# Five PSUM banks in turn for the first-layer sums of an mLSTM and mixture-of-experts kernel

## The chip, the cores and the metric

The kernel runs on one core of a Trainium2 chip. The metric is the device time of one launch in microseconds. A profile comes from one further execution, recorded by the hardware profiler; its span reaches from the first to the last instruction of the core.

## The reference

An mLSTM (4 batches, 8 heads, 768 steps, head size 40) makes 3072 rows of 320 numbers, and a mixture of eight experts is applied to them. Cut to what matters here:

```python
x = attn_out.transpose(0, 2, 1, 3).reshape(B * S, H * D)      # 3072 x 320
expert_idx = argmax(normalised(x) @ normalised(emb).T / tau)   # one expert for each row
for e in range(8):
    mask = expert_idx == e
    h = np.maximum(x[mask] @ w1[e], 0.0)                       # 320 -> 1024, first layer
    out[mask] = gate_w[mask, None] * (h @ w2[e])               # 1024 -> 320, second layer
```

## The kernel before

The order of the instructions on each engine is the order in the source: nothing is reordered, and semaphores are set from the tiles that are read and written. The mLSTM takes about the first third of the span. The expert stage follows; only the mLSTM's last steps overlap it.

**Precision.** Every float32 operand is split into a high and a low part (names ending in `h` and `l`). A product is the sum of three matmuls: high by high, low by high, high by low.

**The stages of the experts.** Two experts are chosen early from a sample. Their tokens come in two lists of 256 each: the first lists (tiles named `_a`) are worked on while the routing still goes on, the second lists (`_b`, 256 columns for each of the two experts) afterwards. The six later experts follow one by one, with 448, 448, 384, 384, 320 and 320 columns. For each expert:

- `gather` has GpSimd fetch the token rows by an indirect DMA (line 322); ScalarE doubles the last 64 columns (`double`, line 352).
- `x_chunk` turns 128 of the row's columns at a time: TensorE transposes (line 360) into a PSUM tile `pt`, ScalarE copies the high part (lines 363, 366), VectorE makes the low part (lines 364, 367). There are three chunks for an expert.
- `mm1` makes one 128-wide slice of the hidden layer: eight matmuls (line 397) into a PSUM tile `ph`, then ScalarE's ReLU into `hh` (line 399), then VectorE's rest into `hl` (line 401, and 405 for an odd half tile). The bank of `ph` comes free after VectorE's instruction. There are eight slices for an expert.
- `mm2` makes the second layer of 128 tokens: 24 matmuls (line 435, or 16 of line 422 for a last half tile) into `po`, scaled by VectorE (line 451) and scattered by GpSimd (line 454).

**The second lists.** While the second layer of the first lists runs, the three turned chunks of the second lists are put between its matmuls, and `g_sums` (line 526) sums the gates in a tile of pool `pM`, which VectorE reads with three instructions (lines 535 to 537). Then sixteen calls of `mm1` follow, eight for each of the two experts. VectorE gets the ordering of the later experts' lists between them, and one-element memsets (line 171) that release the loads of the next expert's weights. Then come four tiles of the second layer, with casts of the next expert's weights (line 208 on ScalarE, line 211 on VectorE) and its turned chunks between them.

**The PSUM pools.** There are eight banks: `pX` has one, `pM` two, `pO` two for `po`, `pH` three for `ph`. `pX` served the mLSTM's transposes and one early tile of the experts and is not used afterwards. `pM` served the routing sums and serves `pt`. Each pool gives its banks out in turn, and an instruction that writes a bank waits until the last reader of its previous tile is done. The lines of the change's inner part are these:

```python
pt = pM.tile([P, 512], F32, name="pt", tag="pm")                                   # x_chunk
ph = pH.tile([P, 512], F32, name="ph", tag="ph")[:, 0 : xc.stop - xc.start]        # mm1
```

Of the kernel before, what the change touches and what calls it, by code (L numbers as in the profile page):

```python
# [11 lines left out]
F32 = mybir.dt.float32  # L12
# [14 lines left out]
P = 128  # L27
# [39 lines left out]
def tile_mlstm_moe(  # L67
# [159 lines left out]
    pX = mctx.enter_context(tc.tile_pool(name="pX", bufs=1, space=PSUM))  # L227
    pM = mctx.enter_context(tc.tile_pool(name="pM", bufs=2, space=PSUM))
# [86 lines left out]
        return [[lambda f=f: next(f)] * k for f, k in parts]  # L315


    pp = []

    def gather_rows(xs, cols, rows=NT + 1):  # L320
        for a, c in enumerate(cols):
# [27 lines left out]
    def double(xs, a, w=P):  # L349

        n = -(-w // P)
        A.copy(xs[:, a : a + n, DM:XW], xs[:, a : a + n, 2 * P : DM])

    def x_chunk(x, xs, c, w=CAP):
        xh, xl, xt = x
        if c == 0:
            double(xs, 0, w)
        pt = pM.tile([P, 512], F32, name="pt", tag="pm")
        for a in range(0, w, P):
            T.transpose(pt[:, a : a + P], xs[:, a // P, c * P : (c + 1) * P], ident)  # L360
        pt = pt[:, 0:w]
        if c < 2:
            A.copy(xh[:, c, 0:w], pt)
            V.tensor_tensor(xl[:, c, 0:w], pt, xh[:, c, 0:w].bitcast(F32), ALU.subtract)
        else:
            A.copy(xt[:, 0:w], pt)
            V.tensor_tensor(xt[L:P, 0:w], pt[L:P], xt[L:P, 0:w].bitcast(F32), ALU.subtract)
# [14 lines left out]
    def hidden(nm):  # L382
        hh, hl = [], []
        for f in range(FC):
            hh.append(mp.tile([P, CAP], F32R, name=f"hh_{nm}_{f}", tag="hh", bufs=FC + 1))
            hl.append(mp.tile([P, CAP], F32R, name=f"hl_{nm}_{f}", tag="hl", bufs=FC + 1))
        return hh, hl

    def mm1(ws, x, xc, f, hs, hc):
        w1h, w1l, (xh, xl, xt) = ws["w1h"], ws["w1l"], x  # L390
        fs = slice(f * P, (f + 1) * P)
        ph = pH.tile([P, 512], F32, name="ph", tag="ph")[:, 0 : xc.stop - xc.start]
        ops = [(w[:, c, fs], xh[:, c, xc]) for c in range(2) for w in (w1h, w1l)]
        ops += [(w1h[:, c, fs], xl[:, c, xc]) for c in range(2)]
        ops += [(w[:, 2, fs], xt[:, xc]) for w in (w1h, w1l)]
        for i, (lt, rh) in enumerate(ops):
            T.matmul(ph, lt, rh, start=i == 0, stop=i == len(ops) - 1)  # L397
        hh, hl = hs[0][f][:, hc], hs[1][f][:, hc]
        A.activation(hh, ph, AF.Relu)  # L399
        full = (hc.stop - hc.start) // P * P  # L400
        V.scalar_tensor_tensor(  # L401
            hl[:, 0:full], ph[:, 0:full], 0.0, hh[:, 0:full].bitcast(F32), ALU.max, ALU.subtract
        )
        if hc.stop - hc.start > full:
            V.scalar_tensor_tensor(
                hs[0][f][:, hc.stop : hc.stop + L], ph[:, full:], 0.0, hh[:, full:].bitcast(F32), ALU.max, ALU.subtract
            )
# [137 lines left out]
    with ExitStack() as actx:  # L545
# [223 lines left out]
        def stage_store(n):  # L769
            j, b = divmod(n, B)  # L770
            SY.dma_start(xrows(j)[:, b], xs_[j][:, b])
# [680 lines left out]
        def do(k):  # L1452
            for _ in range(k):
                if todo:
                    todo.pop(0)()
# [7 lines left out]
        def first_hidden(e, f):  # L1463
            mm1(exps[e]["ws"], xa[e], slice(0, HALF), f, hs, slice(e * HALF, (e + 1) * HALF))
# [12 lines left out]
        n, g = NS - 1, len(GROUPS) - 1  # L1477
        yctx.close()
        pH = mctx.enter_context(tc.tile_pool(name="pH", bufs=3, space=PSUM))
        pp.append(mctx.enter_context(tc.tile_pool(name="pO", bufs=2, space=PSUM, side="right")))  # L1480
        stage_store(n)
        stage_xc(n)
# [26 lines left out]
        def first_out(i, po, ob=None):  # L1509
            e, a = divmod(i, HT)  # L1510
            mm2_out(po, gtf[:, e, a : a + 1], ida_v[i], f"a{i}", ob)
# [51 lines left out]
    for f in g_split:  # L1563
        f()
    xp = x_tiles(mp, "p", CAP)
    xps = [lambda c=c: x_chunk(xp, xs, c) for c in range(3)]
    po2 = first_sum(2, {}, True)
    po3 = first_sum(3, {14: xps[0], 18: xps[1], 22: xps[2]})
# [16 lines left out]
    ranks, places, lists, list_gates, beyond = arrange(mp)  # L1585
    todo += ranks + places + [where] + lists + [tokens] + list_gates
    hs = hidden("b")
    for e in range(NE):
        for f in range(FC):
            mm1(exps[e]["ws"], xp, slice(e * HALF, (e + 1) * HALF), f, hs, slice(e * HALF, (e + 1) * HALF))  # L1590
            do(3 - e)
            if e * FC + f in W2_AT:
                exps[2]["load"](W2_AT.index(e * FC + f), V)()
            if f % 4 == 1:
                first_out(2 * e + f // 4, *first_outs[2 * e + f // 4])
        if e == 0:
            exps[2]["tiles"](wp, 1)
            todo += beyond
    xp = x_tiles(mp, "2", CAP)
    xps = [lambda c=c: x_chunk(xp, xs, c, CAPS[0]) for c in range(3)]  # L1600
    todo += [exps[2]["piece"](*p) for p in PIECES1]
    for i in range(NE * HT):
# [12 lines left out]
    for e in range(NE, E):  # L1615
# [3 lines left out]
        if e + 1 < E:  # L1619
            exp = exps[e + 1] = load_expert(e + 1, at[j + 1])  # L1620
            exp["tiles"](wq if e % 2 == 0 else wp, 1)
            exp["tiles"](w22[(e + 1) % 2], 2)
            todo += [exp["load"](i) for i in range(7)]
            todo += [exp["piece"](*p) for p in PIECES1 + PIECES2]
            n = CAPS[j + 1]
            xs = gather(ids_g[j + 1]) if j else xs_n
            xp = x_tiles(mp, e + 1, CAP)
            xps = [lambda c=c, xp=xp, xs=xs, n=n: x_chunk(xp, xs, c, n) for c in range(3)]
            do(7)
        hs = hidden(e)  # L1630
        for f in range(FC):
            mm1(ws, x, w, f, hs, w)
            do(1)
# [19 lines left out]
    with tc.If(over > 0):  # L1653
        with ExitStack() as octx:
# [49 lines left out]
            with tc.For_i(0, again, 1):  # L1704
                V.tensor_copy(expert, num)
                for n in range(NS):
# [14 lines left out]
                    px = pv.tile([P, 512], F32, name="ovt", tag="ovt")  # L1721
# [33 lines left out]
            with tc.For_i(0, E, 1) as k:  # L1755
# [10 lines left out]
                with tc.For_i(0, NS, 1) as t:  # L1766
# [10 lines left out]
                    pt = pv.tile([P, 512], F32, name="ovt", tag="ovt")  # L1777
# [6 lines left out]
                    for f in range(FC):  # L1784
                        ph = pv.tile([P, 512], F32, name=f"ovh_{f}", tag="ovh")
# [79 lines left out]
```

## Time and profile before

| what | us |
|---|---|
| median of three runs | 335.27 (334.59 to 336.45) |
| the profiled execution | 335.94 |
| its span, first to last instruction | 334.1 |
| TensorE busy in the span | 310.5 |
| VectorE busy | 218.4 |
| ScalarE busy | 162.6 |
| GpSimd busy | 146.8 |

In the rows below, PE is TensorE's matmuls, PEld its weight loads, DVE VectorE, ACT ScalarE, POOL GpSimd. An engine works its instructions off in order, so an instruction that waits holds up all behind it. The arrow in square brackets names what ended the idle time before an instruction, as inferred from semaphores. The end of a matmul in the profile is modelled.

### The profile page before, as it was taken

The page shows a single profiled execution, that of the slowest core. Times are in us where ns is not written, and L with a number is a line of the kernel's source. Part 1 is how long each engine was busy: PE and PEld are TensorE (multiplying, and loading weights), DVE is VectorE, ACT ScalarE, POOL GpSimd, SP SyncE. Part 2 cuts the span into 40 slices and gives each one's busy share as a digit, 9 for nine tenths or more (in the row PEclk, how much of TensorE's full clock was granted, in tenths as well). Part 3 has the DMA queues.
Part 4 walks back from the last instruction along what each step waited for, and adds up shares of the span by engine and source line. Part 5 has one row for each costly group of instructions (what it writes and reads, how often), then busy time and mean ns, then how long its engine had stood idle before and what let it go on. Part 6 is the DMA issues. An engine that isn't in the chain of part 4 may idle for free.

```text
span 334.1 us, 9812 instructions
## 1 busy us (share of the span) xinstructions
PE 310.5 (93%) x3768; PEld 293.1 (88%) x3769; DVE 218.4 (65%) x633; ACT 162.6 (49%) x429; POOL 146.8 (44%) x182
## 2 busy tenths in 40 slices
PE   8997999779987988999889999999999999999992
PEld 4787999769986788999889989999999999999992
DVE  6676797875884649896456596476566585685530
ACT  4666665545654493343245364354454464463410
POOL 6668766768777088040622611240260241332112
PEclk9999999998999899999979999999999999999999
DMA  7999888987998514020592977347347447430001
GB/s 231 278 329 292 260 271 258 344 271 222 284 301 228 204 55 125 2 80 1 186 265 69 257 253 203 110 125 212 118 120 228 126 141 229 115 103 34 17 13 46
DMA packets 29342, 58.54 MB, mean 175 GB/s; under 512 B 3851, under 2 KB 18392, under 8 KB 29286
## 3 DMA queue, kind: packets, MB, share of 16 engines
q1 hardware_dynamic: 26406, 48.91, 47.9%
q0 software_dynamic: 2624, 8.48, 8.4%
q8 instruction: 32, 0.52, 0.6%
q10 hardware_dynamic: 256, 0.43, 0.4%
q14 instruction: 24, 0.20, 0.2%
HBM read 49.98 MB, written 8.19 MB: 174 GB/s over the span
## 4 chain that ended last, share of the span: by engine, by line
PE 79%; DVE 4%; issue 4%; DMA 4%; ACT 3%; POOL 3%; another core or an unknown queue 1%; SPq 1%; POOLq 0%; DVEq 0%; ACTq 0%
PE ph L397 27%; PE po L435 17%; PE s L644 4%; PE po_b L435 4%; PE y L719 4%; PE po_a L435 4%; PE y L730 3%; PE y L681 3%; PE po L422 3%; PE pt L360 2%; DMA sig<-in_og 2%; PE warm L1083 2%; PE px L797 2%; DMA raw<-in_w 2%; PE pm L817 2%
## 5 line engine op out<-in xcount | busy, mean ns | idle before, releaser
L454 POOL DMA_INDIRECT out<-ob,ids x20 | 20.3, 1016 | 99.7 <-DVE ob L451 73.9
L629 POOL TENSOR_TENSOR uv<-kv_s,u_t 64x328 f32<-64x328 f32 x47 | 35.9, 764 | 12.2 <-PE y L681 5.0
L435 PE MATMUL po<-w2h,hh 128*128 128x320 f32 x128 | 40.3, 315 | 0.0
L399 ACT ACTIVATE hh<-ph 128x448 fp32r<-128x448 f32 (+2 forms) x48 | 23.6, 492 | 33.3 <-PE ph L397 31.6
L435 PE MATMUL po<-w2h,hl 128*128 128x320 f32 x128 | 39.6, 309 | 0.0
L435 PE MATMUL po<-w2l,hh 128*128 128x320 f32 x128 | 39.5, 309 | 0.0
L401 DVE SCALAR_TENSOR_TENSOR hl<-ph,hh 128x384 fp32r<-128x384 f32 (+1 forms) x48 | 24.6, 512 | 14.8 <-ACT hh L399 11.7
L397 PE MATMUL ph<-xh,w1h 128*128 128x448 f32 (+2 forms) x96 | 32.2, 338 | 0.1
L397 PE MATMUL ph<-xh,w1l 128*128 128x448 f32 (+2 forms) x96 | 32.1, 337 | 0.0
L208 ACT CAST w1h<-raw 128x512 fp32r<-128x512 f32 x48 | 28.8, 616 | 1.0 <-DMA raw<-in_w 1.0
L451 DVE TENSOR_SCALAR ob<-po,gts 128x320 f32<-128x320 f32 x16 | 8.8, 551 | 28.1 <-PE po L435 28.1
L211 DVE TENSOR_TENSOR w2l<-raw,w2h 128x320 fp32r<-128x320 f32 x58 | 26.5, 493 | 0.2
L644 PE MATMUL s<-q_s,k_e 128*64 128x64 f32 x384 | 24.3, 223 | 1.2 <-DVE w_s L653 1.0
L208 ACT CAST w2h<-raw 128x320 fp32r<-128x320 f32 x62 | 25.2, 461 | 0.0
L397 PE MATMUL ph<-xl,w1h 128*128 128x448 f32 (+2 forms) x96 | 24.6, 337 | 0.0
L322 POOL DMA_INDIRECT xs<-x_d,ids x20 | 21.4, 1071 | 6.9 <-issue 5.5
L211 DVE TENSOR_TENSOR w1l<-raw,w1h 128x512 fp32r<-128x512 f32 x36 | 24.4, 688 | 0.0
L644 PE MATMUL s<-q_s,k_o 128*64 128x64 f32 x384 | 24.2, 222 | 0.0
L435 PEld LDWEIGHTS po<-w2l,hh 128*128 128x128 f32 x128 | 24.1, 188 | 0.0
L653 DVE TENSOR_TENSOR w_s<-s,late 128x512 f32<-128x512 f32 x24 | 16.5, 686 | 11.7 <-PE s L644 7.1
L435 PEld LDWEIGHTS po<-w2h,hh 128*128 128x128 f32 x128 | 24.1, 188 | 0.0
L435 PEld LDWEIGHTS po<-w2h,hl 128*128 128x128 f32 x128 | 24.0, 188 | 0.0
(328 smaller groups left out, 928.9 us busy)
## 6 DMA issues: line engine op xcount, KB each, us to landing
raw<-in_w SPq DMA_DIRECT2D x32, 320.0 KB
kv_s<-in_rows SPq DMA_DIRECT2D x23, 324.0 KB
raw<-in_w SPq DMA_DIRECT2D x14, 512.0 KB
q_s<-in_qt SPq DMA_DIRECT2D x11, 512.0 KB
raw<-in_w SPq DMA_DIRECT2D x18, 256.0 KB
sig<-in_og SPq DMA_DIRECT2D x24, 160.0 KB
x_d<-x SPq DMA_DIRECT2D x24, 160.0 KB
k_e<-in_kt SPq DMA_DIRECT2D x11, 160.0 KB
```

Source lines behind the costliest of these rows:

```text
L208: A.copy(h, src)
L211: (eng or V).tensor_tensor(lo, src, h.bitcast(F32), ALU.subtract)
L322: G.indirect_dma_start(out=xs[0 : c.shape[0], a, 0:DM], out_offset=None, in_=x_d[0:rows], in_offset=bass.IndirectOffsetOnAxis(ap=c, axis=0 ...
L397: T.matmul(ph, lt, rh, start=i == 0, stop=i == len(ops) - 1)
L399: A.activation(hh, ph, AF.Relu)
L401: V.scalar_tensor_tensor(hl[:, 0:full], ph[:, 0:full], 0.0, hh[:, 0:full].bitcast(F32), ALU.max, ALU.subtract)
L435: T.matmul(po[0 : ts_.stop - ts_.start, 0:DM], lt[f][:, ts_], rh[:, f], start=k == 0, stop=k == len(ops) - 1)
L454: store = G.indirect_dma_start(out=out, out_offset=bass.IndirectOffsetOnAxis(ap=slots, axis=0), in_=ob, in_offset=None, bounds_check=NT - ...
L629: (eng[r] if eng else G).tensor_tensor(uv[n % NB][rows, :, :, r], vr_s[q % NB][rows, k], u_t[rows, j, b].unsqueeze(3).broadcast_to([L, 2, ...
L644: T.matmul(s[r * L : r * L + L, c, a], (k_e, k_o)[a % 2][q % NB][:, k, m, cs], q_s[q % NB][:, k, m, cs], start=True, stop=True,)
L653: V.tensor_tensor(w_s[n % NB].rearrange("p c a t -> p (c a) t"), st[n]["s"].rearrange("p c a t -> p (c a) t"), late.unsqueeze(1).broadcast ...
L719: T.matmul(y[c * L : c * L + L, a * 2 * D1 : (a + 1) * 2 * D1], w_s[n % NB][:, c, a], uv[n % NB][:, c, a].rearrange("p r d -> p (r d)"), s ...
```

## The change

`mm1` no longer takes its bank from `pH` alone but from a list that turns with every call. The list holds `pH` once until the second lists begin, so that the first lists have three banks as before; then `pH` is added twice and `pM` twice, which gives the order `pH`, `pH`, `pH`, `pM`, `pM`. `x_chunk` takes its bank from `pX` and `pM` in turn, beginning with `pX`. Nothing else is changed; no instruction of any engine is added or moved in the source.

```diff
-    pp = []
+    pp, banks = [], []
+    turns = [(pM, "pm"), (pX, "px")]
...
-        pt = pM.tile([P, 512], F32, name="pt", tag="pm")
+        turns.append(turns.pop(0))
+        pt = turns[0][0].tile([P, 512], F32, name="pt", tag=turns[0][1])
...
-        ph = pH.tile([P, 512], F32, name="ph", tag="ph")[:, 0 : xc.stop - xc.start]
+        pool, tag = banks[0]
+        banks.append(banks.pop(0))
+        ph = pool.tile([P, 512], F32, name="ph", tag=tag)[:, 0 : xc.stop - xc.start]
...
         pH = mctx.enter_context(tc.tile_pool(name="pH", bufs=3, space=PSUM))
+        banks.append((pH, "ph"))
...
     hs = hidden("b")
+    banks += [(pH, "ph")] * 2 + [(pM, "pm")] * 2
     for e in range(NE):
```

## Rows read from the trace of the kernel before

**Rows 1.** Busy time by engine: us, share of the span, instructions.
```profile
PE 310.5 (93%) x3768; PEld 293.1 (88%) x3769; DVE 218.4 (65%) x633; ACT 162.6 (49%) x429; POOL 146.8 (44%) x182
```

**Rows 2.** By stretch: us; busy (count) PE, PEld, DVE, ACT, POOL; clock, DMA share, GB/s.
```profile
178.00:308.00 130.00, 129.91 (x825) 127.15 (x824) 84.86 (x184) 63.16 (x144) 37.63 (x36) 1.00 0.53 153
```

**Rows 3.** Timeline of TensorE: start us, us, engine, line, what, idle before.
```profile
154.03 0.36 PE L397 MATMUL ph<-xh_p,w1h 128*128 128x256 f32 x1
...
162.41 0.28 PE L397 MATMUL ph<-xt_p,w1l 128*128 128x256 f32 x1
...
163.37 0.28 PE L397 MATMUL ph<-xt_p,w1l 128*128 128x256 f32 x1
...
164.84 0.39 PE L397 MATMUL ph<-xh_p,w1h 128*128 128x256 f32 x1 [0.22 <-DVE hl_b L401]
...
168.48 0.39 PE L397 MATMUL ph<-xh_p,w1h 128*128 128x256 f32 x1 [2.42 <-DVE hl_b L401]
...
173.90 0.31 PE L435 MATMUL po_b<-w2h,hh_b 128*128 128x320 f32 x1
```

**Rows 4.** Timeline of ScalarE, same columns.
```profile
163.94 0.39 ACT L399 ACTIVATE hh_b<-ph 128x256 fp32r<-128x256 f32 x1 [1.77 <-PE ph L397]
167.58 0.94 ACT L399 ACTIVATE hh_b<-ph 128x256 fp32r<-128x256 f32 x3 [3.26 <-remote]
...
174.38 1.65 ACT L208 CAST w1h<-raw 128x512 fp32r<-128x512 f32 x3
175.93 0.40 ACT L352 COPY xs<-xs 128x256 f32<-128x256 f32 x1
```

**Rows 5.** Timeline of VectorE, same columns.
```profile
154.69 0.19 DVE L537 SCALAR_TENSOR_TENSOR gtf<-gtf,pg 128x32 f32<-128x32 f32 x1
...
164.36 0.42 DVE L401 SCALAR_TENSOR_TENSOR hl_b<-ph,hh_b 128x256 fp32r<-128x256 f32 x1 [1.74 <-ACT hh_b L399]
...
168.00 0.42 DVE L401 SCALAR_TENSOR_TENSOR hl_b<-ph,hh_b 128x256 fp32r<-128x256 f32 x1 [2.86 <-ACT hh_b L399]
...
169.06 0.42 DVE L401 SCALAR_TENSOR_TENSOR hl_b<-ph,hh_b 128x256 fp32r<-128x256 f32 x1
```

**Rows 6.** Timeline of GpSimd, same columns: the last of four gathers.
```profile
164.28 1.00 POOL L322 DMA_INDIRECT xs<-x_d,ids x1 [0.30 <-issue]
```

**Rows 7.** Pauses of TensorE and what follows them, columns as in rows 2.
```profile
70.40:72.40 2.00, 0.00 (x0) 0.00 (x0) 1.49 (x6) 0.98 (x4) 0.62 (x1) 1.00 0.83 262
73.60:76.90 3.30, 3.30 (x39) 2.85 (x36) 1.25 (x3) 1.71 (x6) 3.23 (x4) 0.50 0.88 308
105.60:107.60 2.00, 0.67 (x6) 0.32 (x4) 0.00 (x0) 0.12 (x1) 1.70 (x2) 1.00 1.01 193
107.70:111.10 3.40, 3.18 (x30) 2.74 (x31) 1.72 (x5) 0.48 (x2) 1.04 (x1) 0.50 1.06 357
119.10:120.30 1.20, 0.00 (x0) 0.00 (x0) 0.14 (x1) 1.20 (x4) 1.20 (x2) 1.00 0.00 0
120.40:124.40 4.00, 4.00 (x49) 3.97 (x50) 1.93 (x7) 3.97 (x14) 4.00 (x5) 1.00 0.06 10
...
166.10:168.40 2.30, 0.00 (x0) 0.00 (x0) 0.40 (x2) 0.82 (x3) 0.52 (x1) 1.00 1.01 341
169.20:172.50 3.30, 3.30 (x18) 3.30 (x17) 1.85 (x11) 0.77 (x2) 1.00 (x1) 0.50 0.80 181
```

**Rows 8.** Line 397 alone by stretch: us; busy PE, PEld; clock, DMA share, GB/s.
```profile
155.05:161.58 6.53, 6.53 (x58) 6.53 (x57) 1.00 0.07 26
168.48:172.95 4.47, 4.47 (x25) 4.47 (x26) 0.62 0.88 232
```

**Rows 9.** Timeline of TensorE around the gate sums, columns as in rows 3.
```profile
152.41 0.39 PE L435 MATMUL po_a<-w2h,hl_a 128*128 128x320 f32 x1
153.03 1.18 PE L526 MATMUL pg<-ag,op_all 128*128 128x96 f16 x24 [0.22 <-DVE xl_p L364]
```

**Rows 10.** Timeline of ScalarE in a later expert's first layer, columns as in rows 4.
```profile
295.24 0.44 ACT L399 ACTIVATE hh<-ph 128x320 fp32r<-128x320 f32 x1 [0.58 <-PE ph L397]
```

## The prediction

> **What bounds the kernel now.** I read the page's table of busy time first: TensorE is busy for 310.5 of 334.1 us [rows 1]. A share like that can hide where the rest went, so the second view was the busy time by stretch. From 178 to 308 us, which holds nearly all work of the later experts, TensorE is idle for 0.09 of 130 us at full clock [rows 2]: no bank, buffer or weight is waited for there, and a change that only gives room can win nothing in that stretch. The third view was TensorE's timeline around the one stage that the change touches and that has holes, the first-layer sums of the second lists (154 to 174 us). They are sixteen groups of eight matmuls, which I number 1 to 16 (1 to 8 are the first expert's, 9 to 16 the second's). Group 12 starts after a wait of 0.22 us and group 13 after one of 2.42 us, both ended by VectorE's `hl` of line 401 [rows 3], that is by a bank coming free: with three banks, group 12 needs the bank of 9, and 13 that of 10.
>
> The fourth and fifth views say why the banks came free late. The last matmul of group 9 starts at 162.41 and that of group 10 at 163.37, each 0.28 us long [rows 3]; ScalarE reads them at 163.94 and 167.58 [rows 4], 1.2 and 3.9 us after their ends. In those pauses ScalarE had nothing else queued, and at 167.58 it read three groups in 0.94 us: their sums had been there. VectorE follows at 164.36, 168.00 and 169.06 [rows 5]. So TensorE's completions of groups 9 to 12 were seen late. At that time GpSimd's gathers of rows, of which the last of four is issued at 164.28, are in flight [rows 6] and the DMA engines are full (share 1.01) [rows 7]; this is a coincidence in time, not a proven cause. After the long wait the granted clock is 0.50 from 169.2 to 172.5 [rows 7]. [...]
>
> What this stage loses: seven undisturbed groups (2 to 8) take 6.53 us, so 0.933 each [rows 8]. Sixteen from 154.03 would end near 169.1 (the first takes 1.02, to 155.05), and the second layer starts at 173.90 [rows 3]. That is 4.8 us: 0.4 before group 12, 2.6 before group 13, and 4.47 - 2.80 = 1.67 us for groups 13 to 15 at the low clock [rows 8], with 0.1 of small change.
>
> **The change part by part.** It adds and removes no operation on any engine and moves no DMA; it only renames PSUM banks, so what changes is what a group waits for.
>
> *Five banks for `ph` in the second lists.* The ring is three banks of `pH`, then two of `pM`, so group k waits for k-5 instead of k-3. Taking VectorE's and ScalarE's times of groups 9 to 11 as they stand (neither depends on TensorE once the sums are there): group 12 needs 7 and starts at 164.45, 13 needs 8 and starts at 165.38, 14 needs 9, free at 164.36 + 0.42 = 164.78, and starts at 166.32. Group 15 would start at 167.25 but needs 10, free at 168.00 + 0.43 = 168.43 [rows 5]; it starts at 168.48. That leaves a pause of 1.05 us. Group 16 needs 11, free at 169.06 + 0.42 = 169.48, so it starts at 169.54 and ends its stream at 170.5. The second layer then starts 3.4 us sooner than 173.90.
>
> In that sum the clock stays up. Pauses and clock in the same trace: 1.20 us of idleness around 119.1 to 120.3 was followed by 1.00, but 2.00 us around 70.4 to 72.4 and 2.30 us around 166.1 to 168.4 were followed by 0.50 [rows 7]. A pause of 1.05 is nearest to the first, so I take no loss; the other end is 1.67 us and stands as a rival.
>
> *What is late next.* The second layer's first tile reads only halves written by groups 1 to 8, long done, so it can start at 170.5 and end at 174.0. Then the turned rows (line 360) need ScalarE's doubling (line 352, 0.40 us), queued behind three casts of the next expert's weights (1.65 us together), which in turn stand behind the last `hh` [rows 4]. In the new order the last `hh` ends near 171.1, the casts could run to 172.8 and the doubling to 173.2, 0.8 us ahead of need. The casts need the weights' DMA; in the trace they began at 174.38 with nothing left to wait for, so they had landed by then, and no row says how long before. At worst all three start at 174.38, the doubling ends at 176.3 and TensorE waits 2.3 us; at best nothing. The loads were issued well ahead of 171 and the DMA engines work on nothing else of size, so I take 0.2. After that VectorE, ScalarE and the loads follow TensorE, which is the full engine for the whole of 178 to 308 [rows 2], so a shift at 174 should reach the end undiminished.
>
> *Turned rows alternating between `pX` and `pM`.* Before, they alternated between the two banks of `pM`; after, between `pX` (idle since the mLSTM) and one of `pM`. Each third chunk still waits for the first. The gain is one wait: the gate sums (line 526) took the bank of the middle chunk and waited 0.22 us for VectorE's `xl_p` [rows 9]; now they get a bank that has been free for long, and start right behind the transposes. I take 0.2, with 0 as the lower end (the sums before it can hold the queue) and 0.4 as the upper, the distance from the preceding matmul's issue to theirs less one matmul.
>
> *Five banks for the later experts, and turned rows in the same pool.* No group waits for a bank there now [rows 2], so nothing is gained. Late completions occur there too: around 295 us ScalarE sat idle for 0.58 us waiting for TensorE's signal [rows 10], and three banks absorbed it. New waits: the first or second group of an expert may take the bank of turned rows, but these rows have to be evicted before that group can use them as its input anyway. Cost 0, with no row for a gain or a loss.
>
> **The sum.** 3.4 + 0.2 - 0.2 = 3.4 us. The profiled execution took 335.94 us, so it would become 332.5. The median of the runs before is 335.27, 0.67 lower; from that it would be 331.9. I give the middle, 332.2 us.
>
> **The rivals.**
>
> *The clock falls all the same.* The pause of 1.05 us may be enough, as the fall after 105.6 to 107.6 (TensorE busy for 0.67 of 2.00 us there, in pieces) [rows 7] shows that a long unbroken pause is not needed. It costs the 1.67 us that it cost before: 333.9. Against it: the pause at 119.1 cost nothing.
>
> *The completions come when TensorE rests, not when the others do.* The three held completions were seen at 167.58, about 1.5 us after TensorE's queue ran dry at 166.05. If they need that rest, five banks only run it dry later, at 167.4; ScalarE then reads at 168.9, group 10's bank is free near 169.8 in the place of 168.43, the pause is 2.4 us and the clock falls as before. The second layer starts near 171.8, and 1.67 us go to the clock: a gain of 0.4, or 335.2. Against it: group 9's completion was seen at 163.94 while matmuls ran without a break. [...]
>
> *The late completions belong to the recorded execution alone.* Then runs without a recorder never had the wait, and the change is worth its 0.2 us: 335.1. Against it: the recorded execution lies inside the range of the others (334.59 to 336.45), where a loss of 4.8 us should show as a distance. [...]
>
> *Nothing is late.* If the stretch of late completions shortens or falls elsewhere, group 15 doesn't wait either, and 4.8 us or more come back: about 331.
>
> *Slower: a late completion meets the gate sums.* Group 5 now takes the bank that VectorE empties of the gate sums in three reads, the last at 154.69 to 154.88 [rows 5]. It starts at 157.85, so it has 3 us in hand; before, no group waited for this bank. If the 3.9 us of lateness falls on these sums instead of on group 10, group 5 waits 0.9 us, and a second fall of the clock would add 1.67, on top of an undiminished wait later: 337 to 338.5. It decides from a lateness of 3 us at 154 us, when the gathers of this stage have not yet begun, which speaks against it.
>
> **How the numbers follow.** Forecast 0.49 (331.4 to 333.0: the unknown costs are 0 to 2.3 for the casts, taken near the low end, and 0 to 0.4 for the gate sums); nothing late 0.07; the clock falls 0.15; completions need rest 0.12; recorder alone 0.10; slower 0.07. A measurement of this kernel can tell about 0.5%, 1.7 us, so "faster" begins at 333.6. Forecast, nothing late and half of the clock case are below: 0.63. The other half, the rest and the recorder lie within: 0.30. Slower: 0.07. The range from 330.8 to 335.2 leaves out the slower case and the upper edges of two others.
>
> **What would show it.** Right: TensorE's row in 154 to 175 us has one pause of about 1 us or none, ahead of group 15 and not 13; the granted clock stays at 1.00 there; the first second-layer matmul of the second lists starts near 170.3, and every later stage starts 3 to 3.5 us sooner with no new idle time. Wrong: a pause of over 2 us that has only moved by two groups (completions need rest); a clock of 0.50 after a short pause; a wait of the turned rows near 174 for the doubling; or a profile that is faster with times that are not.

## The result, and the profile after

The changed kernel takes 332.06 us (median of ten runs, 330.8 to 336.76). The kernel before, run beside it, takes 335.67 (ten runs, 334.59 to 337.62). The ratio is 0.988, with a 95% interval of 0.9852 to 0.9908: 1.2% faster. The ratio leaves out the changed kernel's run of 336.76 us, which belongs to a slower state (its mean granted clock is 0.979, that of the nine others 0.985 to 0.997). The profiled execution of the changed kernel took 332.36 us, against 335.94 before: 3.58 less, where 3.4 was forecast.

Lines of the expert stage have moved down by one to four: the first-layer matmuls stand at line 401 (397 before), the ReLU at 403 (399), `hl` at 405 (401), the second layer at 439 (435), the gathers at 323 (322). The groups keep their numbers 1 to 16.

From the page of the changed kernel, the span, the busy time by engine, and the granted clock in 40 slices:

```profile
span 330.6 us, 9802 instructions
...
PE 307.4 (93%) x3768; PEld 290.7 (88%) x3769; DVE 220.0 (67%) x633; ACT 162.2 (49%) x429; POOL 146.6 (44%) x182
...
PEclk9999999999999899999999999999999999999999
```

The instruction counts by engine are those of [rows 1]: no work was added or removed. TensorE's share is still 93%, of a shorter span.

TensorE's timeline of the changed kernel (start us, us, engine, line, what, idle before and who ended it), from the gate sums to the first turned rows of the next expert:

```profile
152.56 0.39 PE L439 MATMUL po_a<-w2h,hl_a 128*128 128x320 f32 x1
152.79 1.20 PE L530 MATMUL pg<-ag,op_all 128*128 128x96 f16 x24
...
166.51 0.28 PE L401 MATMUL ph<-xh_p,w1l 128*128 128x256 f32 x1
167.31 0.40 PE L401 MATMUL ph<-xl_p,w1h 128*128 128x256 f32 x2 [0.52 <-issue]
...
168.26 0.39 PE L401 MATMUL ph<-xh_p,w1h 128*128 128x256 f32 x1 [0.31 <-DVE hl_b L405]
...
169.31 0.39 PE L401 MATMUL ph<-xh_p,w1h 128*128 128x256 f32 x1
...
170.37 0.31 PE L439 MATMUL po_b<-w2h,hh_b 128*128 128x320 f32 x1
...
173.90 0.60 PE L362 MATMUL pt<-ident,xs 128*128 128x128 f32 x4
```

The waits of groups 12 and 13 [rows 3] are gone. Group 15, at 168.26, waits 0.31 us for a bank, and group 14 stops in its middle for 0.52 us with no semaphore named ("issue"). The gate sums follow their predecessor without the 0.22 us of [rows 9]. The second layer starts at 170.37 in the place of 173.90.

ScalarE's timeline of the changed kernel, same columns:

```profile
164.43 0.38 ACT L403 ACTIVATE hh_b<-ph 128x256 fp32r<-128x256 f32 x1 [2.48 <-PE ph L401]
167.36 1.49 ACT L403 ACTIVATE hh_b<-ph 128x256 fp32r<-128x256 f32 x5 [2.55 <-PE ph L401]
...
170.85 1.13 ACT L208 CAST w1h<-raw 128x512 fp32r<-128x512 f32 x2
174.34 0.62 ACT L208 CAST w1h<-raw 128x512 fp32r<-128x512 f32 x1 [2.36 <-DMA raw<-in_w]
174.87 0.41 ACT L353 COPY xs<-xs 128x256 f32<-128x256 f32 x1
```

Groups 9 and 10 are again read late, 1.96 and 3.93 us after the modelled ends of their last matmuls. Then five groups, 10 to 14, are read in 1.49 us: the sums of 10 to 13 had been there. The semaphore for which line 403 waits is raised, by the trace's events, at 164.41 us for group 9, at 167.34, 167.43, 167.53 and 167.62 for groups 10 to 13, and at 167.96 for group 14, 0.01 us after its modelled end. In the trace of the kernel before it is raised at 163.91 for group 9 and at 167.56, 167.65 and 167.74 for 10 to 12 (a releaser "remote", as at 167.58 in [rows 4], stands for the same semaphore). So it is the signal that comes late, and ScalarE is not held up by anything of its own. The lateness of group 10 is 3.93 us in both traces, but TensorE was meanwhile filling two more banks.

Stretches of the changed kernel (us; busy and count of PE, PEld, DVE, ACT, POOL; clock; DMA share; GB/s):

```profile
166.80:168.20 1.40, 0.64 (x4) 0.42 (x3) 0.42 (x2) 0.84 (x4) 0.00 (x0) 1.00 1.07 286
169.00:172.50 3.50, 3.50 (x28) 3.46 (x27) 2.93 (x16) 1.80 (x4) 1.90 (x2) 1.00 0.98 232
174.00:304.00 130.00, 130.00 (x831) 127.95 (x830) 85.46 (x185) 64.12 (x146) 37.87 (x36) 1.00 0.56 160
```

The clock stays at 1.00, where it was 0.50 before [rows 7], and the later experts keep TensorE full (130.00 of 130 us), as in [rows 2]. By stages, between the starts of their first matmuls, the second lists' first layer took 16.56 us (19.87 before) and their second layer 15.40 in both. The later experts took 138.06 (138.84) and what follows TensorE's last matmul 6.77 (5.97); these last two cancel. What follows the last matmul varies from 5.61 to 7.08 us in the runs below, with no tie to the banks; of the later experts' 0.78 us, 0.34 are a wait for a bank that is gone (see the part on the later experts).

### The profile page after: what moved, and what is told of

The parts are those of the page before. It is cut to its first block, busy times and chain, and to the rows that moved or that the text cites. A ratio compares the mean times of both kernels' runs of the same rounds, so it can differ in the third digit from the quotient of the medians.

```text
span 330.6 us, 9802 instructions
## 1 busy us (share of the span) xinstructions
PE 307.4 (93%) x3768; PEld 290.7 (88%) x3769; DVE 220.0 (67%) x633; ACT 162.2 (49%) x429; POOL 146.6 (44%) x182
## 4 chain that ended last, share of the span: by engine, by line
PE 76%; DMA 6%; POOL 4%; DVE 4%; ACT 3%; issue 3%; another core or an unknown queue 2%; SPq 1%; POOLq 0%; DVEq 0%; ACTq 0%
PE ph L401 27%; PE po L439 17%; PE po_b L439 4%; PE po_a L439 4%; PE s L648 4%; DMA raw<-in_w 3%; PE y L723 3%; PE po L426 3%; PE y L734 2%; PE pt L362 2%; PE y L685 2%; DMA k_o<-in_kt 2%; PE warm L1087 2%; POOL uv L633 2%
## 5 line engine op out<-in xcount | busy, mean ns | idle before, releaser
L648 PE MATMUL s<-q_s,k_e 128*64 128x64 f32 x384 | 25.3, 223 | 2.5 <-DVE w_s L657 1.2
L648 PE MATMUL s<-q_s,k_o 128*64 128x64 f32 x384 | 24.9, 223 | 1.2 <-issue 1.2
L648 PEld LDWEIGHTS s<-q_s,k_e 128*64 128x64 f32 x384 | 20.7, 137 | 4.0 <-DVE w_s L657 1.6
```

The source lines that it names most:

```text
L648: T.matmul(s[r * L : r * L + L, c, a], (k_e, k_o)[a % 2][q % NB][:, k, m, cs], q_s[q % NB][:, k, m, cs], start=True, stop=True,)
```

## The experiments

The runs below were made in three sets, each on one chip of its own; whether one of these is the chip of the two profiles above isn't recorded. The kernel before ran beside each set: 328.24 us in set one (35 runs), 334.65 in set two (17) and 327.12 in set three (23). A ring of n is a list of n banks that the groups take in turn; a group's lateness is the time from the modelled end of its last matmul to ScalarE's read. The theory (A) is that two more banks bridge late completions. The rivals are that the turned rows' bank brings the gain (B), that the bank count matters in the later experts (D), and, for the lateness itself, that the gathers cause it or that the full DMA engines do.

### Set one: the parts by themselves, and other ring sizes

Turned rows alone:

```diff
-    banks += [(pH, "ph")] * 2 + [(pM, "pm")] * 2
```

> The changed kernel without its ring of five: first-layer sums on three banks everywhere, turned rows still alternating between the mLSTM's bank and one of the routing pool's. Theory A (the gain is the late completions of the second lists, bridged by two more banks): group 13 of the second lists waits about 2.4 us again and the clock falls behind it; the time is that of the kernel before less at most 0.2 us, a ratio of 0.999 to 1.000. Rival B (the gain comes from the turned rows' own banks, along the whole expert stage): most of the 1.2% stays, a ratio of about 0.99.

Measured: 328.30 us, ratio 1.0024 (0.9986 to 1.0063).

The ring of five alone:

```diff
-    turns = [(pM, "pm"), (pX, "px")]
+    turns = [(pM, "pm")]
```

> The changed kernel with its ring of five, but with all turned rows on the routing pool's two banks as before. Theory A: nearly the whole gain, a ratio of 0.988 to 0.990; the second layer of the second lists starts near 170.5 us. Rival B: a ratio of 0.997 or more.

Measured: 327.94 us, ratio 1.0012 (0.9974 to 1.005). The gate sums wait their 0.22 us again.

A ring of four:

```diff
-    banks += [(pH, "ph")] * 2 + [(pM, "pm")] * 2
+    banks += [(pH, "ph")] * 2 + [(pM, "pm")]
```

> The changed kernel with four places in the ring (three banks and one place of the routing pool), so group k waits for k-4. Theory A: group 13 starts without a wait and group 14 waits for group 10, until about 168.3 us; the pause of about 2.1 us lets the clock fall as before. The gain is then 1.0 to 1.3 us (ratio about 0.996); if the clock stays up it is 2.7 us (ratio about 0.992). Rival C (the late completions come only once TensorE rests): the completion of group 10 is seen about 1 us later than in the kernel before, and the ratio is 0.998 to 1.000.

Measured: 327.63 us, ratio 1.0003 (0.9968 to 1.0037).

A ring of six, and three banks again from the later experts on:

```diff
-    banks += [(pH, "ph")] * 2 + [(pM, "pm")] * 2
+    banks += [(pH, "ph")] * 2 + [(pM, "pm")] * 2 + [(pX, "px")]
...
+    banks[:] = [(pH, "ph")]
```

> The changed kernel with the mLSTM's bank as a sixth place of the ring in the second lists, and three banks again for the later experts. Theory A: group 15 no longer waits for group 10, group 16 does and finds it free; 0.3 us to 0.6 us less than the changed kernel, a ratio of 0.986 to 0.987. Rival C: no further gain, since TensorE rests in the end for as long. Rival D (the later experts need their five banks): a loss against the changed kernel, with new idle time of TensorE behind 185 us.

Measured: 327.29 us, ratio 0.9984 (0.9947 to 1.0022).

No ring is worth anything here, and the trace says why: nothing is late on this chip. ScalarE's timeline of the kernel with the turned rows alone, which has the three banks of the kernel before, at groups 9 and 10:

```profile
158.38 0.38 ACT L403 ACTIVATE hh_b<-ph 128x256 fp32r<-128x256 f32 x1 [0.57 <-PE ph L401]
159.34 0.38 ACT L403 ACTIVATE hh_b<-ph 128x256 fp32r<-128x256 f32 x1 [0.58 <-PE ph L401]
```

The sixteen sums of the same kernel as one stretch, columns as above:

```profile
149.70:164.90 15.20, 15.20 (x132) 15.20 (x130) 11.74 (x50) 5.75 (x15) 7.22 (x8) 1.00 0.47 137
```

TensorE is busy for all of 15.20 us. In each of the four kernels the stage takes 15.22, with three banks or six, and every group is read within 0.10 us of its end. The four gathers are issued among groups 7 to 11 here too, the last at 159.93:

```profile
159.93 1.00 POOL L323 DMA_INDIRECT xs<-x_d,ids  x1 [0.31 <-issue]
```

What follows: B falls, as the turned rows alone are not faster here, and in the two profiles above 3.31 us of the gain lie in the sixteen sums. A could not be tested, since its premise is absent. And the sixteen sums need 15.2 us, so the 19.87 of before held 4.65 us of loss, near the 4.8 that the prediction had worked out. The six later experts took 138.06 us in all four, with three, four or five banks, so D finds nothing on this chip.

### Set two: what makes the completions late

The change with three banks again from the later experts on:

```diff
+    banks[:] = [(pH, "ph")]
```

> The changed kernel with five banks in the second lists and three again for the six later experts. Theory A: the same time as the changed kernel within 0.3 us, a ratio of 0.988 to 0.989, and no new idle time of TensorE behind 185 us. Rival D (the later experts need five banks as well): slower than the changed kernel by 0.5 us or more.

Measured: 331.09 us, ratio 0.9919 (0.9876 to 0.9961); the expected 0.988 to 0.989 lies in the interval, but the times can't tell the later experts' part (D) from nothing. On this chip the completions are late. ScalarE's timeline of this kernel at groups 9 to 15:

```profile
164.24 0.38 ACT L403 ACTIVATE hh_b<-ph 128x256 fp32r<-128x256 f32 x1 [1.67 <-PE ph L401]
166.44 0.38 ACT L403 ACTIVATE hh_b<-ph 128x256 fp32r<-128x256 f32 x1 [1.82 <-PE ph L401]
167.90 1.55 ACT L403 ACTIVATE hh_b<-ph 128x256 fp32r<-128x256 f32 x5 [1.08 <-PE ph L401]
```

Groups 9 to 14 are read 0.81 to 2.88 us late. TensorE has no pause among the sixteen groups, which are one stretch here,

```profile
154.50:169.80 15.30, 15.30 (x131) 15.17 (x129) 10.18 (x45) 5.39 (x15) 7.09 (x7) 1.00 0.46 143
```

and the second layer starts 15.43 us after their start at 154.43, 0.21 more than in the undisturbed kernels:

```profile
169.85 0.31 PE L439 MATMUL po_b<-w2h,hh_b 128*128 128x320 f32 x1
```

Five banks bridged this lateness. The next three kernels start from the kernel before, with three banks. The gathers (`tokens`) issued after the last of the sixteen sums:

```diff
-    todo += ranks + places + [where] + lists + [tokens] + list_gates
+    todo += ranks + places + [where] + lists + [lambda: None] + list_gates
...
+    tokens()
```

> The kernel before, with the four gathers of the next expert's rows issued behind the last first-layer sum of the second lists in place of among them. Cause G (the gathers make TensorE's completions late): ScalarE reads groups 9 to 12 within 0.1 us of their ends, and no group waits. Cause W (the weight loads do): groups 9 or 10 to 12 are read 1 to 4 us late as before, and group 13 waits. The turned rows of the next expert come later in either case, so the time as a whole says nothing.

Seven weight loads issued after the last of the sixteen sums, the gathers as before:

```diff
-            if e * FC + f in W2_AT:
-                exps[2]["load"](W2_AT.index(e * FC + f), V)()
...
+    for i in range(7):
+        exps[2]["load"](i, V)()
```

> The kernel before, with the seven loads of the next expert's weights issued behind the last first-layer sum of the second lists. Cause G: completions late as before, group 13 waits 1 us or more. Cause W: every group is read within 0.1 us of its end, and none waits. The casts of these weights come later in either case, so the time as a whole says nothing.

Both of these edits:

> The kernel before, with both the gathers and the loads behind the last first-layer sum of the second lists. If either or both of them are the cause, no completion is late in the second lists and the second layer starts near 169.2 us with the clock at 1.00. If completions are late here too, the cause is neither, and belongs to TensorE's own stream.

Measured: 336.91, 338.37 and 344.97 us, one execution each. Those times mix what the edit does here with what the later transfers cost afterwards, so the stage itself is read. The sixteen sums as one stretch with the gathers later:

```profile
153.20:168.40 15.20, 15.20 (x133) 15.20 (x131) 11.38 (x50) 5.77 (x15) 3.08 (x4) 1.00 0.40 119
```

With the loads later:

```profile
154.50:172.30 17.80, 15.98 (x133) 15.36 (x130) 11.30 (x43) 5.66 (x15) 7.44 (x8) 1.00 0.21 63
```

With both later:

```profile
155.70:170.90 15.20, 15.20 (x133) 15.20 (x130) 11.36 (x43) 5.76 (x15) 3.12 (x4) 1.00 0.09 31
```

With the gathers gone from the stage TensorE loses nothing, at a DMA share of 0.40. With the gathers left and the DMA share down to 0.21, it loses 1.82 us. ScalarE's and TensorE's timelines of the kernel with the loads later:

```profile
163.61 0.38 ACT L399 ACTIVATE hh_b<-ph 128x256 fp32r<-128x256 f32 x1 [0.97 <-PE ph L397]
165.75 0.38 ACT L399 ACTIVATE hh_b<-ph 128x256 fp32r<-128x256 f32 x1 [1.75 <-PE ph L397]
167.92 0.38 ACT L399 ACTIVATE hh_b<-ph 128x256 fp32r<-128x256 f32 x1 [1.79 <-PE ph L397]
169.39 1.06 ACT L399 ACTIVATE hh_b<-ph 128x256 fp32r<-128x256 f32 x3 [1.08 <-remote]
```
```profile
166.64 0.38 PE L397 MATMUL ph<-xh_p,w1h 128*128 128x256 f32 x1 [0.60 <-DVE hl_b L401]
...
168.82 0.39 PE L397 MATMUL ph<-xh_p,w1h 128*128 128x256 f32 x1 [0.96 <-issue]
```

Groups 9 to 13 are read 0.44, 1.62, 2.84, 3.35 and 1.82 us late. Groups 13, 14 and 15 wait 0.60, 0.96 and 0.26 us for their banks, which is the 1.82 lost (the second is shown as "issue", but VectorE was done with group 11, whose bank group 14 takes, at 168.76, just before); for group 13 a wait of 1 us or more had been expected. With the gathers later no group is read more than 0.10 us late, although GpSimd still issues indirect scatters of finished rows (line 454) in the stage, at 157.42, 160.61, 164.74 and 168.32 us. So on this chip, by one execution of each kernel, the lateness of this stage goes with the gathers. Gathers are not enough for it by themselves: in the trace of the kernel before, which has the lateness, three gathers each run among the first-layer groups of the second, third and fourth later experts, and no group there is read more than 0.10 us late. The first of these gathers, and ScalarE's read during it:

```profile
219.83 1.06 POOL L322 DMA_INDIRECT xs<-x_d,ids  x1 [0.33 <-issue]
```
```profile
220.26 0.55 ACT L399 ACTIVATE hh<-ph 128x448 fp32r<-128x448 f32 x1 [0.57 <-PE ph L397]
```

What has to come together with the gathers stays open. Full DMA engines are not needed for it: with the loads later, the fullest two microseconds of the late time are these,

```profile
165.00:167.00 2.00, 1.40 (x12) 1.20 (x11) 0.80 (x4) 0.38 (x1) 1.70 (x2) 1.00 0.58 144
```

at a share of 0.58. The gathers in that later place have a price of their own, seen in TensorE's timeline of the kernel with the gathers later:

```profile
175.39 1.05 PE L360 MATMUL pt<-ident,xs 128*128 128x128 f32 x2 [3.26 <-DMA xs<-x_d,ids]
```

The turned rows now wait 3.26 us for them (and 0.48 more a little later), the granted clock is 0.50 from 175.1 to 178.4 us, and that stage takes 22.54 us in the place of 15.40. Moved there, the gathers cost more than their lateness; no other place was tried.

### Set three: the lateness made by hand

The ring of five alone and the ring of six were taken again, with the edits of set one.

> The changed kernel with its ring of five, all turned rows on the routing pool's two banks. On a chip whose trace shows late completions in the second lists: a ratio of 0.988 to 0.992, since the turned rows' banks are worth at most 0.2 us of the gain. On a chip whose trace shows none (every group read within 0.1 us of its end): 0.998 to 1.002.

> Six places in the ring in the second lists, three banks afterwards. On a chip with late completions: 0.3 to 0.6 us less than with five, a ratio of 0.986 to 0.990. On a chip with none: 0.997 to 1.001.

Measured: 328.06 us, ratio 1.0028 (0.9989 to 1.0067), and 326.95 us, ratio 0.9989 (0.9957 to 1.0021). Nothing is late on this chip either, the stage takes 15.22 and 15.23 us, and nothing is won.

So the lateness was made: eight copies on ScalarE, of a tile whose data nobody needs any more, ahead of the ReLU of group 4. The same edit stands once in the kernel before and once in the changed one:

```diff
+        if held:
+            turned = held.pop()
+            for _ in range(8):
+                A.copy(turned, turned)
...
+            if (e, f) == (0, 3):
+                held.append(turned)
```

`turned` is the tile of the second lists' own rows, which have all been transposed by then.

> The kernel before with a late reading made by hand: ahead of its ReLU of group 4 of the second lists ScalarE copies 384 columns of the old turned-row input onto themselves eight times (about 3.5 us), whatever the chip. Theory A: group 4 is read about 3 us late, group 7 waits for its bank for about 2 us, and the second layer of the second lists starts about 2 us later than without the copies, or 3.5 us if the clock falls as well.

> The changed kernel with the same eight copies. Theory A: group 4 is read as late as in the kernel before with them, but groups 7 and 8 start without a wait and group 9, which needs group 4's bank, waits 0.5 us or less; the second layer starts 1.5 to 3.7 us sooner than there, on any chip. If it starts within 0.5 us of there, two more banks do not bridge a late reading, and theory A falls.

Measured: 332.25 us, ratio 1.0143 (1.0103 to 1.0184), and 331.28 us, ratio 1.0123 (1.0083 to 1.0163), both against the kernel before without copies. In the kernel before, ScalarE reads group 4 at 159.92 us, right behind the copies and 3.66 us late. Its ScalarE and TensorE timelines, and the stretch after the wait:

```profile
155.70 4.31 ACT L402 COPY xs<-xs 128x384 f32<-128x384 f32 x8
```
```profile
160.80 0.39 PE L397 MATMUL ph<-xh_p,w1h 128*128 128x256 f32 x1 [2.66 <-DVE hl_b L405]
```
```profile
161.80:165.00 3.20, 3.20 (x17) 3.20 (x17) 1.73 (x8) 0.77 (x2) 2.43 (x3) 0.50 0.56 169
```

In the changed kernel, where group 4 is read 3.67 us late, TensorE's timeline and the stretch after the wait:

```profile
160.87 0.38 PE L401 MATMUL ph<-xh_p,w1h 128*128 128x256 f32 x1 [0.83 <-DVE hl_b L409]
...
168.64 0.31 PE L443 MATMUL po_b<-w2h,hh_b 128*128 128x320 f32 x1
...
173.74 0.33 PE L362 MATMUL pt<-ident,xs 128*128 128x128 f32 x1 [1.20 <-DMA xs<-x_d,ids]
...
174.29 0.33 PE L362 MATMUL pt<-ident,xs 128*128 128x128 f32 x1 [0.23 <-DMA xs<-x_d,ids]
```
```profile
161.00:164.40 3.40, 3.40 (x29) 3.40 (x30) 3.30 (x16) 1.59 (x5) 2.05 (x2) 1.00 0.29 81
```

This is theory A by itself, with a lateness of known cause; here the reader is held up and not the signal, which for the bank is the same. Group 7 waits 2.66 us with three banks; with five it is group 9, for 0.83. The difference, 1.83, is two groups of 0.93 [rows 8]. After 2.66 the clock is 0.50, after 0.83 it stays at 1.00. The sixteen sums take 19.72 us with three banks and 16.31 with five, 3.41 less. The copies took 4.31 us where 3.5 had been expected, so both waits are longer than expected (about 2 us, and 0.5 or less); the second layer starts 3.33 us sooner, within the expected 1.5 to 3.7.

Of those 3.41 us, 1.0 is seen in the medians (332.25 less 331.28), of six runs each whose ranges overlap (330.89 to 333.0 and 330.57 to 332.13); what is shown is shown by the traces. The trace shows 1.87 given back right behind: the gathers stand behind work that the held ReLUs delay, and start 9.7 us after the first of the sixteen sums (162.03), where the undisturbed one starts them after 6.3 (160.08 in the changed kernel's profile). The second layer now comes sooner, the turned rows wait 1.20 and 0.23 us for their rows, and that stage takes 17.27 us instead of 15.40. The remaining half microsecond lies in the tails of the two executions (5.81 and 6.31), within what they vary by.

## Why the prediction was right, point by point

**What bounds the kernel.** Right. The stage's loss, worked out as 4.8 us, is 4.65 against the 15.22 us of an undisturbed stage. That the late reads and the gathers coincide was called unproven; on one chip the lateness of this stage goes when the gathers go, but other gathers in the same trace bring none. One reading was wrong: the 0.09 us of idleness from 178 to 308 us are a wait for a bank (see the later experts).

**Five banks.** Right in mechanism and size. Group 15 was to start at 168.48, 16 at 169.54 and the second layer at 170.5; they start at 168.26, 169.31 and 170.37. The stage itself shrank by 3.31 us, and 0.22 more came from its earlier start. One thing was not foreseen: most of the pause, 0.52 of 0.83 us, is the stop in the middle of group 14 and not a wait for a bank. It ends at 167.31, when the held signals arrive (167.34); no other trace here has such a stop in this stage, and what it waits for isn't shown. It cost nothing, since group 10's bank was free only at 168.20.

**The clock.** Right in the outcome: it stays at 1.00 after this pause, as after the 1.20 us at 119 [rows 7], and in the kernel with copies (0.83 us, no fall). The step from the length of a pause to the clock is weaker than it looks, and partly luck. In the kernel with the loads later a longer pause, in the first later expert, leaves the clock at 1.00, where 2.42 us in the kernel before were followed by 0.50; TensorE's timeline and the stretch after the pause:

```profile
195.59 0.44 PE L397 MATMUL ph<-xh,w1h 128*128 128x448 f32 x1 [2.80 <-DVE hh L405]
```
```profile
195.60:199.60 4.00, 4.00 (x20) 3.65 (x21) 3.62 (x10) 2.98 (x7) 0.00 (x0) 1.00 0.88 311
```

**The casts and the doubling.** The step failed in its mechanism. It let the turned rows wait for the doubling behind three casts and charged 0.2 us. The third cast did come late, at 174.34 after 2.36 us of waiting for its weights, and the doubling at 174.87; but the turned rows had started at 173.90, right behind the first tile. The first chunk takes columns 0 to 127, while the doubling writes only the last 64, which the third chunk reads. The cost is 0, and its upper bound of 2.3 was bounded by the wrong chunk.

**Turned rows and gate sums.** Right: 0.22 us gained, the stage starts at 153.81 instead of 154.03. It is below what the times can show: alone, on the quiet chip, the ratio is 1.0024 (0.9986 to 1.0063).

**Later experts.** Expected was nothing; the traces show a little. In the fifth of them completions are late too, with three gathers issued from 291.44 to 294.54 us: in the kernel before four groups are read 0.59 to 1.27 us late. Three banks did not absorb that whole, as the prediction has it [rows 10]: TensorE waits for VectorE's last read of a bank. VectorE's and TensorE's timelines of the kernel before:

```profile
296.06 0.21 DVE L405 SCALAR_TENSOR_TENSOR hh<-ph,hh 128x64 fp32r<-128x64 f32 x1
```
```profile
296.02 0.31 PE L397 MATMUL ph<-xt,w1l 128*128 128x320 f32 x1
296.42 0.38 PE L397 MATMUL ph<-xh,w1h 128*128 128x320 f32 x1
```

This group starts 1.43 us after the one before it and the next one 1.25 later, where an undisturbed group takes 1.17: 0.34 us. In the changed kernel the lateness is the same (up to 1.26 us) and every group takes 1.17. The kernel of set two that goes back to three banks loses 0.27 us at this place. So five banks do serve the later experts where completions are late (D), by an amount that the times can't show. The rest of the 138.84 us of before, and of the 138.60 in the kernel that goes back, comes from groups of 1.65 in place of 1.60 us in the first later expert. Five traces have them, all with three banks there, and four other traces with three banks don't; their cause stays open. In the other nine traces the later experts take 138.06 us, with three banks (turned rows alone, copies in the kernel before), with four and with five.

**The other rivals.** That completions wait for TensorE to rest falls. The changed kernel's trace doesn't decide it, since TensorE's stop from 166.79 to 167.31 lies just ahead of the read of group 10 at 167.36 (the rival had expected 168.9); but in the kernel of set two the late completions of groups 9 to 14 all arrive while TensorE runs without a pause. That they belong to the recorded execution alone is not borne out: the times fell by as much as the traces (3.61 us between the medians, 3.58 between the profiled executions), and two chips, recorded in the same way, show no late completion at all. A slower kernel, by a late completion at the gate sums, did not occur: they started at 152.79 us, and the first gather was issued at 160.08.

**What the prediction did not see** is that its premise is not a property of the kernel alone. On two of the three chips of the sets nothing is late in any of the four traces of each (but for the copies), and the rings are worth nothing (ring alone: 1.0012 and 1.0028; ring of six: 0.9984 and 0.9989); on the chip of set two the change, with three banks for the later experts, is worth 0.992, and in the runs of the result 0.988. Why completions are late beside gathers on some chips and not on others stays open. Whether a sixth bank wins more where completions are late was not measured there. No version is shown to beat the changed kernel.

## What to carry to other kernels

Compare, group by group, the modelled end of the producer with the start of its first reader: a lag that the reader's own queue doesn't explain was a late signal here (group 10 of the changed kernel: 3.93 us, read at 167.36, the semaphore raised at 167.34), and the wait behind a ring of banks came to lag + eviction − (banks − 1) × group time: with an eviction of 0.86 us and groups of 0.93 this gives 2.66 and 0.81 for the lags of 3.66 and 3.67 us made by hand, where 2.66 and 0.83 were measured (the 0.86 is fitted to the first, the second is then a test). For the natural lag of 1.62 us of group 10 with the loads later and three banks it gives 0.62, where 0.60 was measured. Before a gain of that kind is counted, look at the same stage on another chip, since the lag, and with it the whole gain, was absent on two of the three chips of the sets (ratios of 1.0012 and 1.0028 for the ring alone). And ask which columns a moved step really reads before you charge it with the wait of the tile's last writer.

## What the hardware showed that was not expected

The chips differ by 2% on the same kernel (328.24 and 327.12 us against 334.65 and 335.67), and part of that lies in two stretches with gathers. One is the stage above. The other is the gathers for the first lists, around 102 to 107 us, where the same code, with four gathers and a DMA share near 1, leaves TensorE half idle in one trace and full in another. First the changed kernel, then the kernel with the turned rows alone on the chip of set one:

```profile
102.60:107.60 5.00, 2.23 (x30) 1.41 (x27) 0.69 (x2) 0.64 (x3) 4.24 (x4) 0.96 1.01 277
```
```profile
102.60:107.60 5.00, 4.98 (x113) 4.40 (x109) 2.64 (x9) 2.91 (x10) 4.08 (x5) 1.00 0.98 278
```

The first of these gathers is issued at 100.96 us in the one and 101.28 in the other, and the first matmul of line 401, of the first lists, starts at 114.9 and 110.8 us, 4.1 us apart. Over all traces that matmul (line 397 in the kernel before) starts at 109.7 to 113.4 us on the two chips where nothing is late and at 114.0 to 116.5 elsewhere, so it varies by nearly as much on chips of one kind. That the gathers cause this second loss too was not tested.
